# A DeltaNet and SwiGLU kernel: compact state, quadrant products on it, a third K buffer and another order of the output products

## The chip, the cores and the metric

The kernel runs on one core of a Trainium2 chip. The metric is the device time of one execution in microseconds (us). Times come from unprofiled runs; beside them stands one execution that the hardware profiler recorded.

The engines are named as the profile names them: PE is TensorE (matrix products), PEld its weight loads, DVE is VectorE, ACT is ScalarE, POOL is GpSimd, SP is SyncE, which here issues nearly all DMA transfers. L728 means line 728 of the kernel.

## The reference

The first half is a DeltaNet layer: for each of 4 x 8 heads a 48 x 48 state runs through 768 time steps. The second half is a SwiGLU network on the 3072 resulting tokens.

```python
k_n = k / (np.linalg.norm(k, axis=-1, keepdims=True) + 1e-06)
for t in range(S):                      # S = 768, D = 48, B = 4, H = 8
    y[:, :, t] = einsum('bhd,bhde->bhe', q[:, :, t], state)
    v_old = einsum('bhde,bhd->bhe', state, k_n[:, :, t])
    state = state + bt * einsum('bhd,bhe->bhde', k_n[:, :, t], v[:, :, t] - v_old)
...
x = attn_out.transpose(0, 2, 1, 3).reshape(B * S, H * D)     # 3072 x 384
xn = x / np.sqrt(np.mean(x * x, axis=-1, keepdims=True) + 1e-06) * rms_g
g = xn @ w_gate                          # 384 x 1536
out = (g * sigmoid(g) * (xn @ w_val)) @ w_out               # 1536 x 384
```

## The kernel before

The sequence is cut into 12 chunks of 64 steps. Within a chunk the recurrence is solved in closed form: the keys are normalised and transposed, their mutual products K K form a triangular matrix, its inverse (scaled by beta) is the matrix M, and then

- R = V - K S, where S is the state at the chunk's start (`ks`, L728, and the two subtractions L736),
- U = M R (`mr`, L761; copied to `u_` by L812 on ScalarE and L814 on VectorE),
- Y = Q S + P U, where P is the masked product Q K (`qs`, L774, and `pu`, L791, in the same PSUM banks),
- S = S + K U (`ku`, L895, and the four additions L904; chunk 0 copies with L906).

Y then gets its root mean square: squares with a running sum on ScalarE (L835), the power on GpSimd (L843 to L845), scaling on ScalarE into `yn` (L850), transposes on TensorE (L860) and the multiplication by `rms_g` on VectorE into `xf` (L863). For the products of the SwiGLU, seven sums of parts of `xf` are made (L881). A corner of `yn`, called `zz`, also serves in the making of M: the product L668 is copied there and read by L690.

All 32 heads are worked on at once. Two heads with even and odd index sit above each other in 64 partitions each; the buffers `kt` and `qt` (transposed K and Q) hold such pairs, and index d in the code is the upper or lower head of a pair. The state `sbd` is block-diagonal: for each pair a 128 x 96 block with the two 48-wide states on its diagonal and zeros off it, so that one product with 128 rows serves both heads. A product with 64 columns and 128 rows (128*64 in the profile) takes half of TensorE's array; one with 64 rows and 64 columns (64*64) takes a quadrant of it. Each fp32 product is two instructions in the profile.

The SwiGLU of chunks 0 and 1 is done plainly (`ffn_plain`, L922 and L940) while the weights are still being converted from 64-bit to 32-bit words on VectorE and ScalarE (L327 to L368, L348). From chunk 2 on a scheme with fewer products is used: `ffn` makes 15 products per half (L1033), collected in `tmp` (L1043 on VectorE, L1045 on ScalarE), with the silu on ScalarE (L1049) and the product into `hf` on VectorE (L1050). `down` then makes seven products (L1089) instead of eight from sums of `hf` and of the output weights: `sums` (L1082) makes s1 (in the tile `xp1`) and s2 (in `tmp`), rewrites a(1,0) in `hf`, and later rewrites s1; products are read by copies `snap` (L1094) and additions `add` (L1098), and stored. x, y and z_ are the three PSUM banks of these products.

The order of the instructions on every engine is fixed when the kernel is built. Each operation is handed to a planner (`P.add`) with an engine, an estimated duration, a priority and the buffers it reads and writes; the planner plays the whole program through once, always taking the operation that can start first and, among those, the one with the lowest priority value, and deals out the eight PSUM banks on the way (`Group`). Priorities are due times from `due(c, lead)`, a chunk's SwiGLU being due at 160 + PERIOD x (c - 2). On the chip nothing is reordered: an instruction that waits holds up everything behind it on its engine. DMA transfers are issued from SP's queue, in that order too.

In the steady part the attention of one chunk is woven into the SwiGLU products of an earlier one.

Of the kernel before, what the change touches and what calls it, by code (L numbers as in the profile page):

```python
# [129 lines left out]
def kernel(  # L130
# [55 lines left out]
    NK, NKQ = 2, 2  # L186
# [25 lines left out]
    sbd = sbt("sbd", [128, 16, 2, D])  # L212
# [35 lines left out]
    PERIOD = 52.5  # L248
# [6 lines left out]
    def setup():  # L255
        for t, key, pr in ((k2[0], ("k2p", 0), 0), (k2[1], ("k2p", 1), 1), (q2, "q2p", 1)):
            P.add("DVE", V(128), lambda t=t: nc.vector.memset(t[:, :, D:DP], 0.0), pr, w=[key])
# [21 lines left out]
        for keys, t in (  # L279
            ([("m1bd", g, bb) for g in range(2) for bb in range(2)], m1bd),  # L280
            ([("x2bd", y_) for y_ in range(4)], x2bd),
            ([("sbd", d, g) for d in range(2) for g in range(2)], sbd),
        ):
            n = 1
            for e in t.shape[1:]:
                n *= e
            P.add("POOL", 0.05 + 0.0009 * n, lambda t=t: nc.gpsimd.memset(t, 0.0), 1, w=keys)
# [140 lines left out]
    def kkeys_(c):  # L428
        return [("k2", c % NK, 0), ("k2", c % NK, 1)]
# [277 lines left out]
    def recur(c):  # L707
# [6 lines left out]
        sk = [("sbd", d, g) for d in range(2) for g in range(2)]  # L714
# [3 lines left out]
        rk = [("r", p) for p in range(2)]  # L718
        if c:
            psk = [Group(), Group()]  # L720

            def ks():
                for p in range(2):
                    for j in range(2):
                        for g in range(2):
                            for bb in range(2):
                                u = 4 * bb + 2 * p + j
                                nc.tensor.matmul(  # L728
                                    psk[p].t[64 * bb : 64 * bb + 64, 0:DM].rearrange("t (j d g e) -> t j g d e", j=2, d=2, g=2)[:, j, g],
                                    kt[ikq][:, u, 64 * g : 64 * g + 64],  # L730
                                    sbd[:, 2 * u + g],
                                )

            P.add("PE", 1.5, ks, pr, r=ktk + sk, w=psk + rk, ps=psk)
            for p in range(2):
                P.add("DVE", V(384), lambda p=p: nc.vector.tensor_tensor(  # L736
                    out=r_[:, 8 * p : 8 * p + 8], in0=vt[:, 8 * p : 8 * p + 8],
                    in1=psk[p].t[:, 0:DM].rearrange("s (h e) -> s h e", e=D), op=ALU.subtract,
                ), pr, r=vk + [psk[p]], w=[("r", p)], last=psk[p])
# [11 lines left out]
        def groups(d, h):  # L751
            return [d[i, h[0]] for i in range(2)]
# [14 lines left out]
        def qs():  # L767
            for p in range(2):
                for j in range(2):
                    for g in range(2):  # L770
                        for bb in range(2):
                            u = 4 * bb + 2 * p + j
                            n = 192 * p + 96 * j
                            nc.tensor.matmul(  # L774
                                psy[g, p].t[64 * bb : 64 * bb + 64, n : n + 96],
                                qt[:, u, 64 * g : 64 * g + 64],
                                sbd[:, 2 * u + g].rearrange("p d e -> p (d e)"),
                                start=(p == 0 and j == 0),
                                stop=False,
                                skip_group_check=True,  # L780
                            )

        def pu(h):
            for p in h:
                for y_ in range(4):
                    for g in range(2):
                        for bb in range(2):
# [7 lines left out]
                                start=(c == 0 and p == h[0] and y_ == 0),  # L795
# [19 lines left out]
        if c == 1:  # L815
            gy = groups(psy, (0, 1))
            P.add("PE", 1.5, qs, pr, r=qk + sk, w=gy, ps=gy)
        for h in halves:
            gy = groups(psy, h)

            def yy(h=h):
                if c > 1:
                    qs()
                pu(h)

            P.add("PE", 0.6 * len(h) + (1.4 if c > 1 else 0.0), yy, py, r=qk + sk + ptk + uk(h), w=gy, ps=gy)
# [3 lines left out]
        for h in halves:  # L830
            gy = groups(psy, h)

            for g in range(2):
                for p in h:
                    P.add("ACT", A(192) + 0.2, lambda p=p, g=g: nc.scalar.activation(  # L835
                        out=yn[:, p, 192 * g : 192 * g + 192], in_=psy[g, p].t[:, 192 * p : 192 * p + 192], func=ACTF.Square,
                        scale=1.0 / math.sqrt(DM), accum_out=ms[i2][:, p, g : g + 1],
                    ), py, r=[psy[g, p]], w=[("yn", p), ("ms", i2, p)], last=psy[g, p])
            cols = slice(h[0], h[-1] + 1)

            def root(cols=cols):
                m = ms[i2][:, cols, 0]
                nc.gpsimd.tensor_tensor(out=m, in0=m, in1=ms[i2][:, cols, 1], op=ALU.add)  # L843
                nc.gpsimd.tensor_scalar_add(m, m, 1e-6)
                nc.gpsimd.tensor_tensor(out=rs[i2][:, cols], in0=m, in1=mhalf[:, cols], op=ALU.pow)  # L845

            P.add("POOL", 1.1, root, py, r=["half"], w=[(k_, i2, p) for p in h for k_ in ("ms", "rs")])
            for g in range(2):
                for p in h:
                    P.add("ACT", A(192), lambda p=p, g=g: nc.scalar.activation(  # L850
                        out=yn[:, p].rearrange("s (y g e) -> s y g e", g=2, e=D)[:, :, g],
                        in_=psy[g, p].t[:, 192 * p : 192 * p + 192].rearrange("s (y e) -> s y e", e=D),
                        func=ACTF.Copy, scale=rs[i2][:, p : p + 1],
                    ), py, r=[psy[g, p], ("rs", i2, p)], w=[("yn", p)], last=psy[g, p])
# [29 lines left out]
        if c < NCH - 1:  # L884
# [12 lines left out]
            P.add("PE", 1.2, ku, py + 2, r=kkeys_(c) + [("k2p", c % NK)] + uk((0, 1)), w=pss + sk, ps=pss)  # L897
            for g in range(2):
                for d in range(2):
                    s = slice(64 * d, 64 * d + 64)  # L900
                    dst = sbd[s, g:16:2, d]
                    src = lambda s=s, g=g: pss[g].t[s, 0:DM].rearrange("s (u e) -> s u e", e=D)
                    if c:
                        P.add("DVE", V(384), lambda dst=dst, f=src: nc.vector.tensor_tensor(out=dst, in0=dst, in1=f(), op=ALU.add), py + 2, r=[pss[g]], w=[("sbd", d, g)], last=pss[g])  # L904
                    else:
                        P.add("DVE", V(384), lambda dst=dst, f=src: nc.vector.tensor_copy(out=dst, in_=f()), py + 3, r=[pss[g], ("xp", 0), ("xp", 1)], w=[("sbd", d, g)], last=pss[g])  # L906
# [164 lines left out]
    def down(c, start):  # L1071
# [42 lines left out]
        product(y, s1, s1k, wsum[:, 0], True, 4)  # L1114
        snap(p5, y, ["p5"])
        sums(a(1, 0), a(0, 0), a(1, 0), ALU.subtract, ak(0, 0), ak(1, 0), 0, 6)
        product(x, s2, s2k, wsum[:, 1], False, 6)
        snap(u2, x, [("tmp", 0)])
        sums(s1, a(0, 1), s2, ALU.subtract, ak(0, 1) + s2k, s1k, 0, 6)
        product(y, s1, s1k, b(1, 1), False, 8)  # L1120
        add(0, 1, u2, y, [("tmp", 0)])
        store(0)
        product(x, a(1, 0), ak(1, 0), b(0, 1), False, 10)
        add(1, 1, p5, x, [("tmp", 2), "p5"])
# [88 lines left out]
```

## Time and profile before

| | us |
|---|---|
| median of 3 runs | 755.35 (754.93 to 755.64) |
| the profiled execution's own time | 754.56 |
| its span, first to last instruction | 752.8 |
| PE busy in the span | 728.9 |
| DVE busy | 588.6 |
| ACT busy | 293.6 |
| POOL busy | 194.0 |
| mean granted TensorE clock | 0.995 of full speed |

Busy times are sums of one engine's instructions. Products on TensorE are pipelined, and the ends of their records overlap with the next start, so the distance from one start to the next says what a batch of products takes. In lists of waits the first name is who waited, the name behind the arrow is who ended the wait, followed by us in total, the number of times and the longest.

### The profile page before, as it was taken

The page shows a single profiled execution, that of the slowest core. Times are in us where ns is not written, and L with a number is a line of the kernel's source. Part 1 is how long each engine was busy: PE and PEld are TensorE (multiplying, and loading weights), DVE is VectorE, ACT ScalarE, POOL GpSimd, SP SyncE. Part 2 cuts the span into 40 slices and gives each one's busy share as a digit, 9 for nine tenths or more (in the row PEclk, how much of TensorE's full clock was granted, in tenths as well). Part 3 has the DMA queues.
Part 4 walks back from the last instruction along what each step waited for, and adds up shares of the span by engine and source line. Part 5 has one row for each costly group of instructions (what it writes and reads, how often), then busy time and mean ns, then how long its engine had stood idle before and what let it go on. Part 6 is the DMA issues. An engine that isn't in the chain of part 4 may idle for free.

```text
span 752.8 us, 22292 instructions
## 1 busy us (share of the span) xinstructions
PE 728.9 (97%) x9538; PEld 670.5 (89%) x9538; DVE 588.6 (78%) x1145; ACT 293.6 (39%) x718; POOL 194.0 (26%) x197
## 2 busy tenths in 40 slices
PE   9999995999999999999999999999999999999996
PEld 8887774877789999999999999999999999999996
DVE  4999999996955975995986896986885986975463
ACT  3425444123334425425425435335345345244231
POOL 5102205143233131331431431332233233100000
PEclk9999998999999999999999999999999999999999
DMA  7848477032344033224224224233233232030000
GB/s 171 213 73 238 126 179 201 1 55 60 64 77 102 1 63 73 45 46 90 44 43 94 44 46 91 44 61 75 52 66 63 54 68 58 13 61 2 22 1 22
DMA packets 206995, 54.60 MB, mean 73 GB/s; under 512 B 199216, under 2 KB 202288, under 8 KB 206896
## 3 DMA queue, kind: packets, MB, share of 16 engines
q1 hardware_dynamic: 201552, 52.19, 32.8%
q10 hardware_dynamic: 5344, 0.98, 0.8%
q8 instruction: 75, 1.23, 0.7%
q14 instruction: 24, 0.20, 0.1%
HBM read 40.83 MB, written 12.32 MB: 71 GB/s over the span
## 4 chain that ended last, share of the span: by engine, by line
PE 79%; DVE 18%; issue 2%; POOL 1%; ACT 0%; DVEq 0%; POOLq 0%
PE bank L1033 35%; PE bank L1089 12%; PE bank L940 7%; PE bank L1179 5%; PE bank L922 3%; DVE acc L593 3%; PE bank L420 2%; DVE acc L587 2%; PE bank L728 2%; PE bank L397 2%; PE bank L774 2%; DVE xp L1082 2%; DVE tmp L1043 2%; PE bank L761 2%; PE bank L690 1%
## 5 line engine op out<-in xcount | busy, mean ns | idle before, releaser
L1033 PE MATMUL bank<-xf,w_in 128*128 128x128 f32 x1440 | 187.1, 278 | 0.4 <-issue 0.4
L1033 PEld LDWEIGHTS bank<-xf,w_in 128*128 128x128 f32 x1440 | 172.1, 192 | 5.1 <-issue 2.0
L1043 DVE TENSOR_TENSOR tmp<-tmp,bank 128x512 f32<-128x512 f32 x180 | 121.8, 685 | 68.9 <-PE bank L1033 51.9
L1033 PE MATMUL bank<-xf,more 128*128 128x128 f32 x960 | 122.9, 276 | 0.3 <-DVE tmp L1043 0.3
L1033 PEld LDWEIGHTS bank<-xf,more 128*128 128x128 f32 x960 | 115.2, 192 | 1.3 <-DVE tmp L1043 0.5
L1045 ACT COPY tmp<-bank 128x512 f32<-128x512 f32 x120 | 70.2, 586 | 108.9 <-PE bank L1033 107.8
L593 DVE TENSOR_REDUCE acc<-acc 128x30 f32<-128x90 f32 (+4 forms) x180 | 85.0, 472 | 6.2
L1049 ACT ACTIVATE tmp<-tmp 128x256 f32<-128x256 f32 x120 | 50.2, 418 | 89.5 <-DVE tmp L1043 89.4
L1050 DVE TENSOR_TENSOR hf<-tmp 128x256 f32<-128x256 f32 x120 | 62.3, 527 | 28.2 <-ACT tmp L1049 27.1
L440 POOL TENSOR_TENSOR knrm<-ksum,half 128x16 f32<-128x16 f32 x12 | 35.3, 2943 | 144.2 <-DVE ksum L439 144.1
L587 DVE TENSOR_TENSOR acc<-acc,at 128x60 f32<-128x60 f32 (+4 forms) x180 | 63.6, 353 | 7.7 <-POOL at L570 4.4
L1089 PE MATMUL bank<-wo_sb,hf 128*128 128x192 f32 x360 | 64.2, 328 | 2.1 <-DVE hf L1050 2.1
L540 POOL TENSOR_TENSOR at<-at,beta_b 128x1024 f32<-128x1024 f32 x10 | 23.6, 2362 | 160.3 <-DMA at<-dkk 160.3
L1089 PEld LDWEIGHTS bank<-wo_sb,hf 128*128 128x128 f32 x360 | 58.3, 190 | 2.9 <-DVE hf L1050 2.5
L1179 PE MATMUL bank<-ident 128*128 128x128 f32 x314 | 40.5, 290 | 1.4 <-POOL ident masks.py:199 1.4
L940 PE MATMUL bank<-xp,w_in 128*128 128x256 f32 x144 | 34.9, 396 | 6.7 <-DVE xp L863 6.7
L1179 PEld LDWEIGHTS bank<-ident 128*128 128x128 f32 x314 | 38.8, 205 | 2.0 <-POOL ident masks.py:199 1.4
L940 PEld LDWEIGHTS bank<-xp,w_in 128*128 128x128 f32 x144 | 28.4, 200 | 12.5 <-DVE xp L863 7.0
L464 POOL TENSOR_TENSOR pt<-pt,mask_p 128x512 f32<-128x512 f32 x20 | 28.0, 1419 | 41.0 <-ACT pt L463 41.0
L922 PE MATMUL bank<-wo_sb,hf 128*128 128x384 f32 x96 | 35.2, 495 | 0.0
L940 PE MATMUL bank<-xf,w_in 128*128 128x256 f32 x144 | 33.8, 382 | 0.0
L940 PEld LDWEIGHTS bank<-xf,w_in 128*128 128x128 f32 x144 | 27.0, 190 | 5.8 <-issue 0.2
(165 smaller groups left out, 1121.1 us busy)
## 6 DMA issues: line engine op xcount, KB each, us to landing
at<-dkk SPq DMA_DIRECT2D x23, 256.0 KB, 3.9
more<-in_moe_w_gate_dram SPq DMA_DIRECT2D x6, 768.0 KB, 5.5
q<-in_q_dram SPq DMA_DIRECT2D x24, 192.0 KB, 4.2
more<-in_moe_w_val_dram SPq DMA_DIRECT2D x6, 768.0 KB, 4.9
vt<-in_v_dram SPq DMA_DIRECT2D x24, 192.0 KB, 3.7
more<-in_moe_w_out_dram SPq DMA_DIRECT2D x6, 768.0 KB, 6.6
out_dram<-tmp SPq DMA_DIRECT2D x48, 96.0 KB, 2.2
k<-in_k_dram SPq DMA_DIRECT2D x23, 192.0 KB, 4.0
```

The costliest lines, as they stand in the source:

```text
L440: P.add("POOL", 2.95, lambda: nc.gpsimd.tensor_tensor(out=knrm[i2], in0=ksum[i2], in1=half, op=ALU.pow), pn, r=[("ksum", i2), "half"], w=[ ...
L587: nc.vector.tensor_tensor(out=acc[:, 1:3, 0:n, j + 2 : W].rearrange("p a i t -> p i a t"), in0=acc[:, old, 0:n, j : j + 2, None].to_broadc ...
L593: nc.vector.tensor_reduce(out=acc[:, new, 0:n, j + 2 : W], in_=acc[:, lo : lo + 3, 0:n, j + 2 : W].rearrange("p a i t -> p i t a"), axis=A ...
L922: nc.tensor.matmul(po[p].t[:, 0:DM], hf[:, spot(f), 128 * p : 128 * p + 128], wo_sb[:, spot(f)], start=(f == f0), stop=(f == f1 - 1), skip ...
L940: nc.tensor.matmul(ps.t[:, TOK * side : TOK * side + TOK], w_in[:, side, h_, 3 * t + i_, n : n + 128], x_[:, 2 * t : 2 * t + 2].rearrange( ...
L1033: nc.tensor.matmul(g.t[:, 128 * z : 128 * z + 128], fac[:, side, 128 * f : 128 * f + 128], xf[:, xs], start=(begin and z == 0), stop=False ...
L1043: P.add("DVE", V(512), lambda t=t, g=g: nc.vector.tensor_tensor(out=t, in0=t, in1=g.t, op=ALU.add), -1, r=[g], w=[tk], last=g)
L1045: P.add("ACT", A(512), lambda t=t, g=g: nc.scalar.copy(t, g.t), -1, r=[g], w=[tk], last=g)
L1049: P.add("ACT", A(256), lambda t=t: nc.scalar.activation(out=t[:, 0:256], in_=t[:, 0:256], func=ACTF.Silu), -1, w=[tk])
L1050: P.add("DVE", V(256), lambda t=t, f0=f0, p=p: nc.vector.tensor_tensor(out=hf[:, spot(f0) : spot(f0) + 2, 128 * p : 128 * p + 128], in0=t[ ...
L1089: nc.tensor.matmul(g.t[:, 0:192], a_[:, f], b_[:, f], start=(begin and f == 0), stop=(f == 5), skip_group_check=True)
L1179: nc.tensor.matmul(warm[:, 0:128], ident, ident)
```

## The change

- The state is kept in `state`, 128 x 16 x 48, without the zeros: the upper head of a pair in partitions 0 to 63, the lower in 64 to 127. K U is added to it by two operations on 128 partitions instead of four on 64.
- K S and Q S are one function, `on_state`: for each pair and head a product of 64 rows and 64 columns on 48 elements, going round the four quadrants; the results of the upper and lower heads lie in two PSUM banks, and `by_d` picks the matching columns.
- Q S is its own operation with its own two banks. ScalarE copies it into `yn`, and the result of P U is added there by VectorE. From chunk 1 on the squares read `yn`, two of 384 elements instead of four of 192, the scaling is two operations within `yn`, and GpSimd adds no partial sums.
- K has three buffers instead of two.
- PERIOD goes from 52.5 to 50.5.
- In `down` the seven products and their sums come in another order.

```diff
-    NK, NKQ = 2, 2
+    NK, NKQ = 3, 2
-    sbd = sbt("sbd", [128, 16, 2, D])
+    state = sbt("state", [128, 16, D])
-    PERIOD = 52.5
+    PERIOD = 50.5
...
-            psk = [Group(), Group()]
-            def ks():
-                ...
-                nc.tensor.matmul(
-                    psk[p].t[64 * bb : 64 * bb + 64, 0:DM].rearrange(...)[:, j, g],
-                    kt[ikq][:, u, 64 * g : 64 * g + 64],
-                    sbd[:, 2 * u + g],
-                )
-            P.add("PE", 1.5, ks, pr, r=ktk + sk, w=psk + rk, ps=psk)
+            psk, psq = [Group(), Group()], [Group(), Group()]
+            def on_state(t, ps):
+                for x_ in range(4):
+                    for g in range(2):
+                        for d in range(2):
+                            for bb in range(2):
+                                rows, u, n = slice(64 * d, 64 * d + 64), 4 * bb + x_, 96 * x_ + 48 * g
+                                nc.tensor.matmul(
+                                    ps[d].t[64 * bb : 64 * bb + 64, n : n + 48],
+                                    t[rows, u, 64 * g : 64 * g + 64],
+                                    state[rows, 2 * u + g],
+                                )
+            P.add("PE", 1.1, lambda: on_state(kt[ikq], psk), pr, r=ktk + sk, w=psk + rk, ps=psk)
...
+            P.add("PE", 1.1, lambda: on_state(qt, psq), pr, r=qk + sk, w=psq, ps=psq)
+            for d in range(2):
+                P.add("ACT", A(384), lambda d=d: nc.scalar.copy(
+                    by_d(yn.rearrange("s p n -> s (p n)"), d), psq[d].t[:, 0:DM].rearrange("s (x n) -> s x n", x=4)
+                ), py, r=[psq[d]], w=[("yn", p) for p in range(2)], last=psq[d])
...
-        def qs():
-            ...
-            def yy(h=h):
-                if c > 1:
-                    qs()
-                pu(h)
-            P.add("PE", 0.6 * len(h) + (1.4 if c > 1 else 0.0), yy, py, r=qk + sk + ptk + uk(h), w=gy, ps=gy)
+            P.add("PE", 0.6 * len(h), lambda h=h: pu(h), py, r=ptk + uk(h), w=gy, ps=gy)
...
+                for g in range(2):
+                    P.add("DVE", V(384), lambda g=g: nc.vector.tensor_tensor(
+                        out=yn...[:, :, g], in0=yn...[:, :, g],
+                        in1=gy[g].t[:, 0:DM].rearrange("s (y e) -> s y e", e=D), op=ALU.add,
+                    ), py, r=[gy[g]], w=[("yn", p) for p in range(2)])
+                for p in range(2):
+                    P.add("ACT", A(384) + 0.2, lambda p=p, gy=gy: nc.scalar.activation(
+                        out=gy[p].t[:, 0:DM], in_=yn[:, p], func=ACTF.Square, scale=1.0 / math.sqrt(DM), accum_out=ms[i2][:, p, 0:1],
+                    ), py, r=[("yn", p)], w=[gy[p], ("ms", i2, p)], last=gy[p])
...
+                for p in range(2):
+                    P.add("ACT", A(384), lambda p=p: nc.scalar.mul(yn[:, p], yn[:, p], rs[i2][:, p : p + 1]), py, ...)
...
-                for d in range(2):
-                    s = slice(64 * d, 64 * d + 64)
-                    dst = sbd[s, g:16:2, d]
+                dst = state[:, g:16:2]
...
         product(z_, a(0, 1), ak(0, 1), b(1, 0), True, 2)
         add(0, 0, p1, z_, [("tmp", 0)])
-        product(y, s1, s1k, wsum[:, 0], True, 4)
+        product(x, s2, s2k, wsum[:, 1], False, 4)
+        snap(u2, x, [("tmp", 0)])
+        product(y, s1, s1k, wsum[:, 0], True, 6)
         snap(p5, y, ["p5"])
         sums(a(1, 0), a(0, 0), a(1, 0), ALU.subtract, ak(0, 0), ak(1, 0), 0, 6)
-        product(x, s2, s2k, wsum[:, 1], False, 6)
-        snap(u2, x, [("tmp", 0)])
         sums(s1, a(0, 1), s2, ALU.subtract, ak(0, 1) + s2k, s1k, 0, 6)
-        product(y, s1, s1k, b(1, 1), False, 8)
+        product(x, a(1, 0), ak(1, 0), b(0, 1), False, 8)
+        add(1, 1, p5, x, [("tmp", 2), "p5"])
+        product(y, s1, s1k, b(1, 1), False, 10)
         add(0, 1, u2, y, [("tmp", 0)])
         store(0)
-        product(x, a(1, 0), ak(1, 0), b(0, 1), False, 10)
-        add(1, 1, p5, x, [("tmp", 2), "p5"])
         product(x, a(1, 1), ak(1, 1), wsum[:, 2], False, 12)
```

In the profile of the old kernel the seven products of one `down` appear by their tiles: `wo_sb,hf` (a(0,0), then a(0,1)), `wsum,xp` (s1), `wsum,tmp` (s2), `wo_sb,xp` (the rewritten s1), `wo_sb,hf` (a(1,0)) and `wsum,hf` (a(1,1)).

In the changed kernel as built, the planner puts Q S right behind K S in most chunks, and K S of a chunk in chunks 3, 5 and 8 to 11 soon behind K U of the chunk before: K U, the products Q K, one to three batches of the SwiGLU, K S, Q S. In the kernel before some ten batches lie between the two.

## The prediction

> **What bounds the kernel now.** I read the page first: busy shares, then the chain that ended last.
>
> ```profile
> PE 728.9 (97%) x9538; PEld 670.5 (89%) x9538; DVE 588.6 (78%) x1145; ACT 293.6 (39%) x718; POOL 194.0 (26%) x197
> ...
> PE 79%; DVE 18%; issue 2%; POOL 1%; ACT 0%; DVEq 0%; POOLq 0%
> ```
>
> TensorE is busy almost all the time and carries the chain; VectorE carries 18% of it. The windows by stage say where each of them does so (columns: length, then busy time of PE, PEld, DVE, ACT, POOL):
>
> ```profile
> 83.80:129.83 46.03, 37.31 (x584) 29.03 (x582) 44.60 (x69) 21.84 (x49) 14.61 (x11) 0.97 0.65 162
> 129.83:216.70 86.87, 86.87 (x780) 68.43 (x781) 74.62 (x146) 20.48 (x54) 28.24 (x27) 0.98 0.24 45
> ...
> 502.70:557.77 55.07, 54.21 (x781) 52.31 (x782) 44.70 (x90) 23.50 (x59) 17.10 (x18) 1.00 0.32 61
> ```
>
> Up to 129.83 us VectorE is full (44.60 of 46.03) and TensorE has holes. From there on TensorE is full, and a steady period of one chunk is 55.07 us long with 54.21 of TensorE work. The waits of TensorE from 129.8 us on are short enough to list:
>
> ```profile
> PE bank L940 <- DVE xp L863: 6.7, 1, 6.7
> PE bank L1089 <- DVE xp L1082: 5.0, 6, 0.9
> PE bank L1089 <- DVE hf L1050: 2.1, 2, 1.1
> PE bank L1089 <- DVE tmp L1098: 0.4, 1, 0.4
> ```
>
> The first is the end of the startup (TensorE restarts at 129.83 when chunk 1's x is there); the second is six waits, one per chunk, for the third `sums` of `down`. So after 129.83 a microsecond taken from TensorE's list, or from these waits, comes off the end, unless a new wait takes it back. The price of a batch is read from starts in TensorE's timeline, not from busy times, which overlap:
>
> ```profile
> 502.63 1.54 PE L728 MATMUL bank<-sbd,kt 128*64 128x96 f32 x32
> 504.10 1.16 PE L1033 MATMUL bank<-xf,w_in 128*128 128x128 f32 x8
> ...
> 521.83 1.15 PE L761 MATMUL bank<-r,mt 64*64 64x48 f32 x64
> 522.91 1.16 PE L1033 MATMUL bank<-xf,w_in 128*128 128x128 f32 x8
> ...
> 524.89 1.54 PE L774 MATMUL bank<-sbd,qt 128*64 128x96 f32 x32
> 526.36 1.15 PE L791 MATMUL bank<-u,pt 64*64 64x48 f32 x64
> 527.33 1.11 PE L895 MATMUL bank<-u,k 64*64 64x48 f32 x64
> 528.37 1.09 PE L397 MATMUL bank<-ident,q 128*128 128x128 f32 x8
> ...
> 540.97 2.19 PE L1089 MATMUL bank<-wo_sb,xp 128*128 128x192 f32 x12 [0.86 <-DVE xp L1082]
> ```
>
> K S (L728) and Q S (L774) take 1.47 us each from start to next start; 64 instructions of 64x48 in quadrants take 1.08 (L761, after full-array products), 0.97 (L791) and 1.04 (L895).
>
> **Quadrant products.** Each of K S and Q S becomes 64 instructions of 64x48, the very form and quadrant order of L791. K S, behind full-array products, is priced like L761: 1.08. Q S follows K S as built, so like L791 and L895: 1.0. P U loses its neighbour and becomes the first quadrant batch: 0.97 to 1.08, a loss of 0.11. After the restart there are ten K S (chunks 2 to 11): 10 x 0.39 = 3.9. Nine Q S: 9 x 0.47 = 4.2. P U: 10 x 0.11 = 1.1 back. The tenth Q S, of chunk 2, no longer waits for P U of its own chunk; as built it stands ahead of chunk 1's transposes (L860), in the 6.7 us hole, and its whole 1.47 leaves the full stretch. Sum: 3.9 + 4.2 - 1.1 + 1.47 = 8.5. Bounds: all new batches at 1.09 (L420, 64 instructions) gives 7.7; all at 0.97 and no loss on P U gives 11.0. I take 8.5, as L761, L791 and L895 are the same shape.
>
> A rule speaks against this part. The Trainium skill, TensorEngine Tiling (Array Packing), section Instruction Overhead, says that a matmul has about 60 cycles of overhead, so that a short free dimension costs as much as 60, and not to take the tiling factor from a dimension that is already small. By it twice the instructions at 48 would cost 64 x 60 against 32 x 96, 1.25 times as much: an estimate of 1.84 us a batch instead of 1.47, and 7 us lost over the nineteen batches. The rows of L791 and L895 have the very shape, and go by 1.0, so the sum stays with the rows.
>
> **Order of the output products.** Before, the product on the rewritten s1 (`wo_sb,xp`) stands 1.95 us after the last reader of s1 (`wsum,xp`), and VectorE needs the 0.94 us rewrite behind queued work: 0.86 of wait. As built, `wo_sb,hf` on a(1,0) now lies between, with `wsum,tmp` ahead of `wsum,xp`. VectorE's queue between (two L863 at 0.55, some L881 at 0.43, one step of the inverse at 1.0, the rewrite 0.94) ends about 0.8 us before its reader. So the 5.0 goes, and so does the 0.4 at the very end (L1098 read the bank that the last product writes; another product lies between now). The price is that `wsum,tmp` is due one product earlier and needs s2; its last third, the only part that waits for the last tiles, starts 1.3 us into the product, and I cost that at nothing (0 to 4 us over all chunks). One of the two L1050 waits (1.0, first SwiGLU chunk) goes too, since another product, a weight product and the transposes lie between now. Sum: 6.4, bounds 3 to 6.5.
>
> **Compact state.** Two state additions on 128 partitions replace four on 64 (L904, 0.55 each: it is elements per partition that count), and two additions of Q S to P U (about 0.55, like L736) come. VectorE per chunk: -1.1 + 1.1 = 0. ScalarE gets two copies of 384 (0.48, L812), two squares and two scalings of 384 instead of four each of 192 (0.33 + 0.21 and 0.43): about +0.5 us, and it is busy 23.5 of 55.07. GpSimd loses one 0.28 addition. The chain from P U to the transposes of y grows by the two additions: additions 1.2, squares 1.4, GpSimd 1.0, scalings 1.0, with hand-overs some 5.5 us, and as built 7 to 8 us of TensorE work lie over it. Setup swaps a GpSimd memset for a small VectorE one, under the K load: 0, at most 0.2 if uncovered. In the full VectorE stretch before 129.83, chunk 0's four copies become two, chunk 1's four additions two, and two come: -1.1. But GpSimd's mask products and its scaling of `at` run there and stretch two-input VectorE work:
>
> ```profile
> 122.74 2.98 DVE L333 SCALAR_TENSOR_TENSOR wo_sb<-more,wo_sb 128x768 uint32<-128x768 uint32 x1
> 125.76 1.97 DVE L338 TENSOR_SCALAR more<-wo_sb 128x768 uint32<-128x768 uint32 x1
> ```
>
> (0.96 and 0.56 elsewhere). As built the masks come ahead of `at`, so up to 2 us more of the conversions fall under GpSimd. I take -0.5 for the restart, bounds -1.5 to +2.
>
> **Third K buffer.** It moves two DMA issues on SP's queue and the norms earlier, past no new issue of another kind. TensorE waits for no K in the list above: 0. The new PERIOD only shifts due times; what it does is in the built order.
>
> **New waits.** As built, three places are short. In chunk 5's `down`, the product on a(0,1) comes 2.0 us after its last SwiGLU product, and addition 0.69, silu 0.42, product 0.42, with one more L1043 and two steps of the inverse queued ahead, need 3.1: +1.1 (0 to 2). Chunk 6's transposes stand only 3.9 us ahead of its SwiGLU, and VectorE needs two L863, seven L881 (2.5 together), a step of the inverse and an L1098: +1.9 (0 to 2.5). Chunk 11's stand one product (1.95) ahead, with 3.6 of VectorE work: +1.5 (0.5 to 2). And in six chunks (3, 5, 8 to 11) K S now follows K U after 2 to 4 us of other products, while the state additions queue behind the additions of y and the norm's sum (L437, 0.95): I find 0.2 us of slack, cost +0.1 each, 0.6 in all (0 to 6). Sum +5.1.
>
> **Sum.** -8.5 - 6.4 - 0.5 + 5.1 = -10.3. The profiled execution took 754.56 (span 752.8, 1.8 around it), so 744.3 there; the runs' median is 755.35, 0.8 above it, and 745.0 is my number.
>
> **Rivals.** (a) The new waits don't come, because VectorE has room where I queued it: -8.5 - 6.4 - 0.5 = -15.4, 740. For it: VectorE is idle 10 us a period; against: 12.1 of 13 us busy just behind K U in the steady period. (b) The reorder is given back: waits for s2, hf and xf grow to twice my sum and the order gains half: -8.5 - 3.2 - 0.5 + 10.2 = -2, 753. For it: every one of TensorE's late waits already names VectorE. (c) Slower: K S waits for the state. In those six chunks the additions of the state stand behind work that itself waits for P U, the norm's sum and GpSimd-stretched hf products (0.42 rising to 1.56 at the worst). It decides when VectorE comes to the y additions more than 2 us later than P U's end: each chunk then loses 1.8 us or more, 6 x 1.8 = 11, and the gain is gone; at 2.5 us each, 15, with (b)'s half gain of the order and the other new waits (4.5), it ends 7 above the median, near 762. Against: the queue ahead of them is some 3.2 us and starts 2.9 us before P U ends. (d) Nothing changes on TensorE, quadrants being limited per instruction at L728's 46 ns: L791 at 15 ns excludes this.
>
> **Chances.** My sum 0.54, (a) 0.18, (b) 0.19, (c) 0.08, (d) 0.01. The measurement tells 0.2% (1.5 us) from no change. Faster: all of my sum and (a), and most of (b): 0.87; same 0.05; slower 0.08. The range goes from just under (a), 739.0, to inside (b), 751.5; the unknown bounds (7.7 to 11.0, 0.5 to 10 of waits) fit into it.
>
> **What would show it.** Right: L728 and L774 as 64 instructions with starts 1.0 to 1.1 apart, a steady period near 53.4 us, no wait for the third `sums` in the new order, waits of 1 to 2 us for hf in chunk 5 and for xf ahead of chunk 6's and 11's SwiGLU, the restart at 128 to 131. Wrong: K S waiting for the state in each of the six chunks, batches at 1.4 or more, or a restart past 132.

## The result and the profile after

The changed kernel takes 758.2 us (median of 20 runs, 754.6 to 761.1) against 754.8 for the kernel before (20 runs, 753.4 to 756.8): ratio 1.0046, 95% interval 1.0032 to 1.0060. A second series (experiment e12) gives 1.0049 (1.0028 to 1.0070). It is slower by 0.5%, where 745 was forecast. Two executions that took far longer than the rest, one of e16 (1883 us) and one of e17 (1456 us), are in no ratio.

The page of the first profiled execution (754.73 us, span 753.0), the same two lines as of before:

```profile
PE 720.5 (96%) x10212; PEld 661.8 (88%) x10212; DVE 593.9 (79%) x1146; ACT 297.0 (39%) x674; POOL 189.8 (25%) x185
...
PE 68%; DVE 25%; issue 4%; POOL 2%; ACT 1%; DVEq 0%; POOLq 0%
```

TensorE's busy time is 8.4 us less. But its share of the chain fell from 79% to 68%, and VectorE (18% to 25%) and "issue" (2% to 4%) took it over. Two steady periods, in the windows by stage, hold less work in about the same time:

```profile
494.88:549.84 54.96, 53.32 (x844) 51.68 (x843) 44.97 (x91) 24.11 (x55) 16.41 (x16) 1.00 0.32 62
549.84:605.42 55.58, 53.58 (x843) 51.45 (x843) 45.55 (x90) 23.98 (x55) 16.43 (x16) 1.00 0.25 47
```

53.4 was forecast for the period, 55.07 was the old one. Line numbers of the changed kernel differ from the old ones: L728 is now both K S and Q S, L770 is M R, L784 P U, L896 K U, L419 Q K, L939 `ffn_plain`, L1032 `ffn`, L1088 `down`; on VectorE L903 adds to the state, L1042 to `tmp`, L1049 makes `hf`, L1081 are the `sums`. The next view is the string of quadrant batches in TensorE's timeline of the first profile:

```profile
530.18 1.15 PE L784 MATMUL bank<-u,pt 64*64 64x48 f32 x64
531.15 1.11 PE L896 MATMUL bank<-u,k 64*64 64x48 f32 x64
532.08 1.11 PE L419 MATMUL bank<-qt,kt 64*64 64x64 f32 x58
534.39 0.34 PE L419 MATMUL bank<-qt,kt 64*64 64x64 f32 x6 [1.20 <-issue]
...
535.75 1.15 PE L728 MATMUL bank<-state,kt 64*64 64x48 f32 x64
536.72 0.98 PE L728 MATMUL bank<-state,qt 64*64 64x48 f32 x50
538.13 0.44 PE L728 MATMUL bank<-state,qt 64*64 64x48 f32 x14 [0.43 <-issue]
```

K S starts 0.97 before Q S, less than the 1.08 that was forecast. Q S, at the end of the string, takes 1.78 to the next start (538.50), more than the old 1.47. Twice TensorE stops in the middle of a batch, and the profile shows nothing that it waits for ("issue").

That first profile is one of the fastest runs. The second (e12, span 757.8) is nearer the median, and its waits of TensorE from the restart on are:

```profile
PE bank L939 <- DVE xp L864: 4.3, 1, 4.3
PE bank L1088 <- DVE xp L1081: 3.3, 4, 1.4
PE bank L419 <- issue: 3.1, 3, 1.3
PE bank L1088 <- DVE hf L1049: 2.9, 3, 1.3
PE bank L1032 <- DVE tmp L1042: 2.4, 2, 1.2
PE bank L728 <- issue: 2.0, 4, 1.0
PE bank L728 <- DVE state L903: 1.7, 2, 1.2
PE bank L784 <- DVE u L807: 1.4, 1, 1.4
```

From these lists and the windows, in us (waits below 0.15 are in no list):

| | before | after, first profile | after, second |
|---|---|---|---|
| restart at | 129.83 | 126.23 | 130.16 |
| restart to end | 623.0 | 626.8 | 627.6 |
| TensorE busy in it | 610.1 | 604.1 | 602.3 |
| "issue" waits in it | 0.4 | 5.2 | 5.1 |
| waits for the third sums | 5.0 | 1.9 | 3.3 |
| all other listed waits | 3.2 | 10.8 | 12.1 |

By the second profile: 7.8 less work, 4.7 more "issue", 1.7 less for the third sums, 8.9 more of other waits: +4.1 of the 4.6 that the stretch grew. Busy time also grows where the granted clock is at half, which it is for 4.0 us of the stretch before, 6.8 of it in the first profile and 3.4 in the second. Taking off half of these, an estimate, leaves 7.4 and 7.5 less work in the two.

### The profile page after: what moved, and what is told of

Its sections match the earlier page's. It is cut to its first block, busy times and chain, and to the rows that moved or that the text cites. A ratio compares the mean times of both kernels' runs of the same rounds, so it can differ in the third digit from the quotient of the medians.

```text
span 753.0 us, 23603 instructions
## 1 busy us (share of the span) xinstructions
PE 720.5 (96%) x10212; PEld 661.8 (88%) x10212; DVE 593.9 (79%) x1146; ACT 297.0 (39%) x674; POOL 189.8 (25%) x185
## 4 chain that ended last, share of the span: by engine, by line
PE 68%; DVE 25%; issue 4%; POOL 2%; ACT 1%; DVEq 0%; POOLq 0%
PE bank L1032 33%; PE bank L1088 14%; DVE acc L592 4%; DVE acc L586 3%; PE bank L939 3%; DVE hf L1049 3%; PE bank L1178 2%; PE bank L419 2%; DVE tmp L1042 2%; PE bank L396 2%; PE bank L921 2%; PE bank L728 2%; PE bank L689 1%; PE bank L770 1%; DVE w_in L332 1%
## 5 line engine op out<-in xcount | busy, mean ns | idle before, releaser
L1042 DVE TENSOR_TENSOR tmp<-tmp,bank 128x512 f32<-128x512 f32 x180 | 122.4, 685 | 80.9 <-PE bank L1032 66.8
L1032 PE MATMUL bank<-xf,w_in 128*128 128x128 f32 x1440 | 182.1, 277 | 0.4 <-ACT tmp L1044 0.4
L1032 PEld LDWEIGHTS bank<-xf,w_in 128*128 128x128 f32 x1440 | 170.0, 192 | 4.3 <-issue 1.4
L1032 PE MATMUL bank<-xf,more 128*128 128x128 f32 x960 | 125.4, 277 | 2.4 <-DVE tmp L1042 2.4
L1032 PEld LDWEIGHTS bank<-xf,more 128*128 128x128 f32 x960 | 115.6, 192 | 4.3 <-DVE tmp L1042 2.8
L1049 DVE TENSOR_TENSOR hf<-tmp 128x256 f32<-128x256 f32 x120 | 70.6, 591 | 19.5 <-ACT tmp L1048 18.2
L1088 PE MATMUL bank<-wo_sb,hf 128*128 128x192 f32 x360 | 66.0, 334 | 3.7 <-DVE hf L1049 3.3
L586 DVE TENSOR_TENSOR acc<-acc,at 128x60 f32<-128x60 f32 (+4 forms) x180 | 66.4, 369 | 3.4
L1088 PEld LDWEIGHTS bank<-wo_sb,hf 128*128 128x128 f32 x360 | 59.9, 194 | 5.0 <-DVE hf L1049 4.0
L1178 PE MATMUL bank<-ident 128*128 128x128 f32 x284 | 37.2, 291 | 1.4 <-POOL ident masks.py:199 1.4
L1178 PEld LDWEIGHTS bank<-ident 128*128 128x128 f32 x284 | 35.5, 205 | 2.5 <-POOL ident masks.py:199 1.4
L939 PE MATMUL bank<-xp,w_in 128*128 128x256 f32 x144 | 34.6, 395 | 3.1 <-DVE xp L864 3.1
L939 PEld LDWEIGHTS bank<-xp,w_in 128*128 128x128 f32 x144 | 28.3, 198 | 9.0 <-DVE xp L864 3.3
L613 POOL COPY acc<-acc 128x128 f32<-128x128 f32 x40 | 16.4, 448 | 72.3 <-DVE acc L592 72.3
L939 PE MATMUL bank<-xf,w_in 128*128 128x256 f32 x144 | 34.2, 383 | 0.0
L1093 ACT COPY tmp<-bank 128x192 f32<-128x192 f32 x30 | 9.4, 318 | 57.9 <-PE bank L1088 50.6
```

The lines of the kernel that those rows point to most:

```text
L586: nc.vector.tensor_tensor(out=acc[:, 1:3, 0:n, j + 2 : W].rearrange("p a i t -> p i a t"), in0=acc[:, old, 0:n, j : j + 2, None].to_broadc ...
L939: nc.tensor.matmul(ps.t[:, TOK * side : TOK * side + TOK], w_in[:, side, h_, 3 * t + i_, n : n + 128], x_[:, 2 * t : 2 * t + 2].rearrange( ...
L1032: nc.tensor.matmul(g.t[:, 128 * z : 128 * z + 128], fac[:, side, 128 * f : 128 * f + 128], xf[:, xs], start=(begin and z == 0), stop=False ...
L1042: P.add("DVE", V(512), lambda t=t, g=g: nc.vector.tensor_tensor(out=t, in0=t, in1=g.t, op=ALU.add), -1, r=[g], w=[tk], last=g)
L1049: P.add("DVE", V(256), lambda t=t, f0=f0, p=p: nc.vector.tensor_tensor(out=hf[:, spot(f0) : spot(f0) + 2, 128 * p : 128 * p + 128], in0=t[ ...
L1088: nc.tensor.matmul(g.t[:, 0:192], a_[:, f], b_[:, f], start=(begin and f == 0), stop=(f == 5), skip_group_check=True)
```

## The experiments

Theories, by the names used in the expectations: T1, strings of quadrant batches outrun the supply of instructions. T2, VectorE comes late for what the new order and the new additions ask of it. T3, the shorter PERIOD spoils the planner's order. T5, waits halve TensorE's granted clock for a while. Where the planner's costs or rules are touched, the whole built order moves.

**One part alone, or one part undone (e1 to e4).**

e1 is the kernel before with only the `down` hunk of the change.

> The kernel before with the new order of the seven output products and nothing else (block-diagonal state, two K buffers, PERIOD 52.5 stay). Theory T1, instruction supply: what ate the gain is strings of quadrant batches (P U, K U, Q K, K S, Q S) that outrun the instructions; this kernel keeps the 32 wide products for K S and Q S, so it should bring my full term for the order: the 5.0 us of waits for the third sums and 0.4 at the end go, no more 'issue' waits than before's 1.8 us in all, and the median falls by 4 to 6.5 us against the kernel before (ratio 0.991 to 0.995). Theory T2, VectorE comes late: the new order asks for s2, hf and the last output sum earlier, and the waits for them grow by what the old one lost: ratio 0.998 to 1.004, with 4 us or more of waits for hf, s2 and the adds in the list.

Measured 759.4, ratio 1.0045 (1.0027 to 1.0064): the order alone makes it slower. Its profile, TensorE and then VectorE in one steady `down`:

```profile
594.54 2.11 PE L1089 MATMUL bank<-wsum,xp 128*128 128x192 f32 x12
596.49 2.11 PE L1089 MATMUL bank<-wo_sb,hf 128*128 128x192 f32 x12
599.08 2.19 PE L1089 MATMUL bank<-wo_sb,xp 128*128 128x192 f32 x12 [0.48 <-DVE xp L1082]
```

```profile
596.72 1.01 DVE L863 TENSOR_TENSOR xf<-bank,g_sb 128x384 f32<-128x384 f32 x2
...
597.98 0.95 DVE L1082 TENSOR_TENSOR xp<-hf,tmp 128x768 f32<-128x768 f32 x1
```

The rewrite of s1 may start when `wsum,xp` has read it, about 596.6, and its reader is due at 598.4. The rewrite ends at 598.93, 0.5 too late. One product lies between the two, as in the kernel before, with `wsum,tmp` there (`wsum,xp` at 536.04, `wsum,tmp` at 537.99, reader at 540.97). The reader moved back by one product and so did the last read. These waits total 4.2 instead of 5.0, and those for the additions L1098 and for L1043 grew from 0.7 to 2.3.

e2 is the changed kernel with the old product order and:

```diff
-    NK, NKQ = 3, 2
+    NK, NKQ = 2, 2
-    PERIOD = 50.5
+    PERIOD = 52.5
```

> The changed kernel with the old order of products, two K buffers and PERIOD 52.5, so the compact state with quadrant K S and Q S alone. In the built order only a few chunks have five quadrant batches in a row (K S stands 5 or more SwiGLU products behind K U in all but the last chunk). T1: the quadrant price is right (K S and Q S 1.0 to 1.1 instead of 1.47) and little is lost to supply: 'issue' waits below 4 us after 126 us of the span, the five waits for the third sums (about 5 us) still there; ratio 0.986 to 0.993 (8.5 for the quadrants, 3 from the earlier restart, less 1 to 2). T2 (the additions of Q S and the state load VectorE at the wrong places): waits for state, xf and hf grow by 6 us or more here too; ratio 0.996 to 1.004.

Measured 766.0, ratio 1.0144 (1.0118 to 1.0169), worse than either theory said. In its built order the products of `down` wait for the additions that read their bank:

```profile
PE bank L1088 <- DVE tmp L1097: 9.3, 7, 2.6
```

and the restart comes at 134.67, after waits of 1.35 for the state, 2.8 for yn and 6.2 for chunk 1's x, with the clock at half from 123.1 to 140.2. The work itself is 7.0 shorter after the restart (603.1 against 610.1).

e3 undoes only the product order, e4 only PERIOD (52.5).

> The changed kernel with the old order of the seven products; state, third K buffer and PERIOD 50.5 as changed. The five quadrant batches stand in a row in chunks 8 and 11 only; Q S still follows K S at once. T1: the waits for the third sums come back (+5 us), and some 2 to 3 us of 'issue' waits go: ratio to the kernel before 1.005 to 1.010. T2, the new order is what makes VectorE late: the waits for hf, state and the sums go with it, ratio 0.990 to 0.998.

> The changed kernel with PERIOD 52.5 as before; all else as changed. Theory T3, the shorter period makes the planner push attention ahead, into the shadow of the SwiGLU of the chunk before, and this makes K S wait for the state and the strings: at 52.5 the ratio to the kernel before falls under 0.997, with state waits under 1 us. T1 and T2: the built order has as many strings (K S two products or less behind Q K in chunks 3, 5, 7, 9 and 11), so the time stays within 2 us of the changed kernel's, ratio 1.002 to 1.007.

Measured 765.1, ratio 1.0124 (1.0106 to 1.0142), and 766.6, ratio 1.0142 (1.0122 to 1.0162). Neither lies in a range that T1 or T2 gave. T3 has the wrong sign: with the other parts in place, the new order and PERIOD 50.5 are worth some 6.9 and 8.4 us by the medians. In e3 the waits for hf are 8.0 in all, in e4 the "issue" waits 7.9 after the restart (13.4 in the whole span). So in these orders no part is good or bad by itself; each built order has its own set of waits.

**Instruction supply (e8, e6, e9).**

e8 appends products to the kernel before:

```diff
+        for w_, n in ((48, 1024), (96, 512)):
+            for i in range(n):
+                d, bb, x_ = i % 2, i // 2 % 2, i // 4 % 4
+                nc.tensor.matmul(banks[6 + d][64*bb : 64*bb+64, 96*x_ : 96*x_+w_], kt[0][64*d : 64*d+64, 4*bb + x_, 0:64], ...)
```

> The kernel before with products appended after its last one, on operands that lie ready, results used by nobody: 1024 quadrant products of 64x48, then 512 of 64x96. T1: the first 100 to 200 of the short ones go at 15 ns each, then instruction supply sets in at about 27 ns (256 instructions, 128 products, per 16 KB fetch of 3.4 to 4.1 us), so the 1024 take 26 to 30 us with 'issue' waits; the 512 wide ones go at about 31 ns, 16 us, without such waits. Rival (no supply limit): 15 ns throughout, 15.5 to 17 us for the 1024 and as much for the 512.

e8 was run once. The expectation counted products where the profile has two records for each; its prices are those of a record. Measured:

```profile
747.68 3.59 PE L1186 MATMUL bank<-r,kt 64*64 64x48 f32 x230
752.25 2.08 PE L1186 MATMUL bank<-r,kt 64*64 64x48 f32 x128 [0.97 <-issue]
...
810.53 2.87 PE L1186 MATMUL bank<-r,kt 64*64 64x96 f32 x128 [0.60 <-issue]
```

230 records go at 15.6 ns, then 128 at a time, a new lot every 3.47 to 4.02 us: 27 to 31 ns a record. 128 records with their weight loads are 256 instructions, one 16 KB packet of the instruction queue, and in the trace each hole ends some 1.2 to 1.5 us after such a packet lands. T1's mechanism holds, and the wide products, against the expectation, are held back too (22.4 ns each when they run, but 3.47 to 3.75 us per lot). Five batches in a row are 320 records.

e6, same order, K S and Q S in half as many records:

```diff
-                    for g in range(2):
...
-                                nc.tensor.matmul(ps[d].t[..., n : n + 48], t[rows, u, 64 * g : 64 * g + 64], state[rows, 2 * u + g])
+                            nc.tensor.matmul(ps[d].t[..., 96 * x_ : 96 * x_ + 96], t[rows, u, 0:64], state[rows, 2 * u : 2 * u + 2])
```

> The changed kernel, same order on every engine, but K S and Q S go as 32 quadrant products on 96 elements instead of 64 on 48: half the instructions for the same streamed columns (the odd heads take their neighbour's keys, so this leaves part of the computation out). T1: the strings are five batches long as before but hold 256 fewer instructions of 1280 in fifths, so 'issue' waits after the restart fall from 6.8 to 3.5 us or less, starts of K S and Q S stay about 1.0 apart, and the median falls by 2.5 to 5 us, to 753 to 756. Rival: the 'issue' waits are semaphores or banks that the profile does not show; they stay at 5 to 8 us, and the median within 1.5 us of 758.

Measured 752.6, ratio 0.9967 (0.9949 to 0.9984):

```profile
535.02 0.89 PE L727 MATMUL bank<-state,kt 64*64 64x96 f32 x32
535.73 0.84 PE L727 MATMUL bank<-state,qt 64*64 64x96 f32 x32
536.50 1.09 PE L396 MATMUL bank<-ident,q 128*128 128x128 f32 x8
```

This proves less than was meant: a batch of 32 wide records takes 0.71 to 0.83 from start to start, not 1.0, so some 5 of the 5.6 us are plain work. The holes in K S and Q S (3.5 in the first profile) are gone; those in Q K, ahead of them in the string, are not. The "issue" sum after the restart is 4.9, and not the 3.5 or less that T1 said.

e9 teaches the planner the supply:

```diff
+                    if e == "PE" and s > 130.0:
+                        s = max(s, t_tok + (need(op) - tok) / 33.0)    # need: 64 for a quadrant batch
```

> The changed kernel with one rule more in the planner, and nothing else: a batch of 64 quadrant instructions may start only when a store of 105 instructions, refilled at 33 per us, holds 64 (as measured in the string experiment: 128 per 3.6 us). From chunk 2 on the built order then has P U, K U, one to three products of the SwiGLU or the output, Q K, another one or two, K S, Q S. T1: 'issue' waits after the restart fall from 5.2 us to 1.5 or less, and the median falls by 3 to 5 us, to 753 to 755.5. Rival (the holes only cover other waits): the 'issue' waits go, but waits for state, hf or xp grow by as much, median 757 or more.

Measured 764.4, ratio 1.0128 (1.0109 to 1.0146). The strings are broken and the "issue" waits after the restart fall from 5.2 to 1.5, as T1 said. The rival has the time: waits that the changed kernel does not have come in (lines stand 7 lower here: L1095 is a product of `down`, L871 the multiplication into xf, L868 the transposes of y),

```profile
PE bank L1095 <- DVE xf L871: 4.9, 3, 2.6
...
PE bank L868 <- ACT yn L862: 1.5, 1, 1.5
```

and behind two of them (1.95 and 2.57 us) the clock halves.

**VectorE relieved (e5, e7, e13, e14; e15 to e17).** The first four cut the seven sums of xf to 4 columns from chunk 3 on, in the changed kernel, in e1, in e9 and in the kernel before:

```diff
-                    out=dst, in0=a, in1=b_, op=op
+                    out=dst[..., 0:w_], in0=a[..., 0:w_], in1=b_[..., 0:w_], op=op     # w_ = 4
```

> The changed kernel, every instruction in the same order on every engine, but the seven sums of parts of xf (L881, 2.5 us of VectorE per chunk) run on 4 of 128 columns from chunk 3 on, so about 1.8 us less of VectorE per chunk just where its queue is full; this leaves part of the computation out. T2 (VectorE comes late): the waits for hf, xp, tmp and state after the restart, 14.6 us in the changed kernel's profile (5.0 + 3.3 + 3.3 + 2.5 and 0.5 for u; 3.1 of them the restart itself), fall to 6 us or less, and the median falls by 4 to 8 us to 750 to 754. T1 (instruction supply): the 'issue' waits of 6.8 us stay within 1.5 us of that, and the median falls by less than 3 us.

> The kernel before with the new order of products alone (759.4 us), same order of instructions, with the sums L881 cut to 4 columns from chunk 3 on (part of the computation left out). T2: the new order gains nothing because VectorE is full in the stretch of the output products and the rewrite of s1 comes as late as the order asks for it; with 1.8 us a chunk less there, the waits for the third sums fall from 4.2 (plus 1.3 for L1098 and 1.0 for L1043) to under 1.5 in all and the median to 750 to 754. T1 and T5 (the clock): the waits hardly fall, 757 or more.

> The kernel of the supply experiment (planner with the store of instructions) with the sums L881 cut to 4 columns as in the light experiment (part of the computation left out): both sinks relieved. If each sink only hands its time to the other: 'issue' waits 1.5 us or less after the restart, waits for VectorE 10 us or less (15.4 in the changed kernel, about 20 in the supply experiment), median 748 to 753, 5 us or more under the changed kernel's 758. Rival (neither is what holds the kernel; the loss is in chains of latency through PSUM banks, ScalarE and VectorE, whatever the queue's length): VectorE waits 13 us or more, median 755 or more.

> The kernel before with the sums L881 cut to 4 columns from chunk 3 on (part of the computation left out). With the same cut the new order of products took 752.6 us. If the order is worth its 5 us where VectorE has room, this kernel keeps its waits for the third sums and stays at 755 to 758. If VectorE's queue was the cause of those waits, they go here too (5.0 to under 1.5 us), the median is 749 to 752.5, and the order is worth nothing or less in either case.

Measured 756.9, 752.6, 761.0 and 752.9 us; ratios 1.0014 (0.9996 to 1.0031), 0.9959 (0.9947 to 0.9972), 1.0075 (1.0049 to 1.0101) and 0.9960 (0.9944 to 0.9975). The relief was put in the wrong place. In e14 the reader of the third sums still waits 4.7 in all, since only one of the seven sums stands ahead of the rewrite in VectorE's queue. What two of the four do show: with this relief the order of products alone is worth nothing (e7's 752.6 against e14's 752.9).

The last three cut the steps of the inverse, which do stand ahead of it, in the changed kernel, in the kernel before and in e9's:

```diff
-            def step(j=j, n=n, m=m):
+            def step(j=j, n=1 if c >= 3 else n, m=m):
```

> The changed kernel, same order of instructions, with the steps of the inverse from chunk 3 on cut to one row block instead of up to 15 (part of the computation left out), some 6 us less of VectorE per chunk. If VectorE's lateness eats the gain: its waits after the restart fall from 15.4 to 7 us or less, the 'issue' waits stay near 5, and the median falls by 5 to 9 us to 749 to 753. Rival (chains of latency): waits for VectorE stay at 11 or more, median 755 or more.

> The kernel before with the same cut of the inverse (part of the computation left out). Its waits for the third sums (5.0) stand behind these steps and go, to 1 us or less; median 749 to 752. With e15 this gives the worth of the whole change where VectorE has room: the shorter work of TensorE (8) less instruction supply (4.7) says that e15 is 1 to 4 us faster than this; if e15 is no faster, the change is worth nothing even then.

> The kernel of the supply experiment with the same cut of the inverse (part of the computation left out): strings broken up and VectorE relieved. If these two are all that eats the gain: 'issue' 1.5 us or less, VectorE waits 8 or less after the restart, median 744 to 749, 3 us or more under e15. Rival: the order that the planner makes here is what costs (its waits of 2 to 2.6 us for xf ahead of the product on s1, which ScalarE's scaling of yn makes late): 753 or more.

Measured 750.3 (ratio 0.9941, 0.9922 to 0.9959), 748.2 (0.9905, 0.9886 to 0.9924) and 748.3 (0.9911, 0.9895 to 0.9927). The changed kernel's list after the restart in e15, then that of e16:

```profile
PE bank L1088 <- DVE hf L1049: 2.8, 4, 1.1
PE bank L419 <- issue: 2.8, 3, 1.1
PE bank L728 <- issue: 2.3, 4, 0.7
PE bank L728 <- DVE state L903: 2.0, 2, 1.2
```

```profile
PE bank L1089 <- DVE hf L1050: 1.9, 2, 1.1
PE bank L1089 <- DVE xp L1082: 0.7, 1, 0.7
```

The third sums are gone from e15's list and nearly from e16's: VectorE's queue made those waits. The lighter queue took 7.8 us off the changed kernel (758.0 to 750.3), but 6.8 off the kernel before as well, so the change stays 2 us behind. What is left in e15 is above all instruction supply (5.1) and two waits as long as in the second profile: hf, through ScalarE's silu (2.8 against 2.9), and the state behind K U (2.0 against 1.7). e17 takes the supply out too (0.9), and is 2.0 us faster than e15: breaking up the strings pays where VectorE has room. But it is no faster than e16. TensorE's busy time after the restart is 9.3 less there than in e16 (600.6 against 609.9), and waits other than for supply are 10.2 against 3.0, with these at the head of e17's list:

```profile
PE bank L1095 <- DVE hf L1056: 3.7, 4, 1.3
PE bank L791 <- DVE u L814: 1.9, 2, 1.2
PE bank L1095 <- DVE xf L871: 1.6, 2, 0.8
PE bank L868 <- ACT yn L862: 1.4, 1, 1.4
PE bank L1095 <- DVE state L910: 1.3, 3, 0.6
```

So with both relieved, waits along chains through VectorE and ScalarE still take the gain.

**The clock (e10, e11, e12).** In the first profile of the changed kernel the granted clock is at half from 365.36 to 368.77, right after a wait of 1.48 for hf; the product behind it took 3.90 instead of 2.1. e10 and e11 put useless products into waits of the changed kernel (at the restart, and in chunks 4 and 11 ahead of the product on a(0,1)) and of the kernel before (at the restart):

```diff
+                    for z in range(8 if c == 1 and f == 0 and side == 0 else 0):      # e11: 22
+                        nc.tensor.matmul(ps.t[:, 128 * (z % 4) : 128 * (z % 4) + 128], ident, ident)
```

> The changed kernel, same order, with useless products of 128x128 on the identity put into three waits: 8 before chunk 1's first product at the restart (3.1 us of wait), 5 before the product on a(0,1) of chunk 4 (1.5 us of wait), 4 before that of chunk 11 (1.1). Theory T5: a wait of 1.5 to 3 us halves the granted clock for 3.4 us or a multiple, 1.7 us of loss each; with the waits filled the profile shows no half clock at chunk 4 and at most 3.4 us of it around the restart, the mean clock of the runs rises from 0.992 to 0.995 or more, and the median falls by 1.5 to 4 us. Rival (the clock falls for another reason): mean clock unchanged within 0.001, median the same or up to 1 us more for the products that come too late.

> The kernel before with 22 useless products of 128x128 (about 4.9 us) in its wait of 6.7 us ahead of chunk 1's first product. T5: the half clock from 127.0 to 133.8 us of the span goes, of which 4.0 us lie behind the restart, so the median falls by 1.5 to 2.2 us (ratio 0.997 to 0.998), the mean clock rises by 0.004. Rival: the products delay the restart or the clock falls all the same: ratio 0.999 to 1.003.

> The changed kernel as it is, for a second profile and the spread of its runs on this chip: ratio to the kernel before 1.003 to 1.007 as before. T1 and T5 say that its runs differ among themselves by the number of windows of half clock, each 1.7 us and 0.0023 of mean clock, and by the length of the hole in the string of chunk 1 (1.6 us in the first profile, 3.2 to 3.9 in three variants that hold the same string): runs of clock 0.995 and more at 754 to 757, of 0.991 and less at 758 to 761.

e10: 760.4, ratio 1.0078 (1.0065 to 1.0091), clock 0.991 to 0.995: missed, and 2.3 us slower than e12, the changed kernel in the same series. There was no half clock at chunk 4, but e12 had none there either without any filling; the clock fell at 118.1 instead, within the hole of 4.3 us in chunk 1's string, and once more at 165.9. e11: 753.2, ratio 0.9986 (0.9974 to 0.9998), clock 0.996 to 1.000, no half clock but at the end: a gain of 1.1 us, somewhat less than the 1.5 to 2.2 expected, and the only version here, with the whole computation, below the kernel before. e12: clock alone does not sort the changed kernel's runs (at 0.995 they lie from 755.9 to 759.5), while in e1 it does: 756.5 to 756.6 at 0.995, 759.4 to 761.0 at 0.991 to 0.993. The other part of the spread is in e12's own timeline of chunk 1:

```profile
120.22 0.78 PE L896 MATMUL bank<-u,k 64*64 64x48 f32 x20 [3.40 <-issue]
...
130.16 5.19 PE L939 MATMUL bank<-xp,w_in 128*128 128x256 f32 x15 [4.26 <-DVE xp L864]
```

The packet of instructions that ends this hole landed at 118.8; in the first profile the one with the same place in the queue had landed at 113.7, and the restart came at 126.23. Of the ten other profiles with this string all but e2's have the hole, at 3.2 to 4.3 us.

## Why the prediction was wrong

By the second profile the span grew by 5.0 us where 10.3 less was forecast. Of these 15.3, new waits on other lines have 5.2, instruction supply 4.7, the third sums 3.3, the restart 0.8 and TensorE's work 0.7; 0.6 is in no list.

- **Quadrants: right about the work, with a term left out.** The sum put 8.5 on the stretch after the restart; busy time there fell by 6.0 in the first profile and 7.8 in the second (7.4 and 7.5 with the clock taken off, as above). K S was priced at 1.08 and is 0.97. The 1.0 for Q S holds for a batch whose instructions are there; at the end of the string above Q S costs 1.78, and 2.33 in the second profile. The prediction took its rows from batches that stand two or three together, and asked of its 128 instructions, twice as many as before, only what they do to the array. Their supply was put at nothing without a reason; it is 4.7 us.
- **The rule that was set aside.** The Trainium skill, TensorEngine Tiling (Array Packing), section Instruction Overhead, says that a product with a free dimension of 1 takes as long as one with 60. e8 agrees in kind: a record takes 16.3 ns with 48 elements and 22.4 with 96, so the short one costs 0.73 of the long one and not half. The comparison that mattered, against 46 ns for the old 128-row form, still went as the prediction said.
- **Product order: the step whose mechanism failed.** The -6.4 rested on another product lying between s1's last reader and the reader of its rewrite. But `wsum,tmp`, which lay there before, had moved ahead of `wsum,xp`: one product between them in both orders. VectorE's rewrite was to end 0.8 us ahead of its reader; in e1 it ends 0.5 after the reader is due. Of the 5.0, 3.3 stayed in the second profile (1.9 in the first, 4.2 in e1), and with the order alone the kernel got slower.
- **New waits: less than half of their size, and other places.** 5.1 was forecast, or 3.7 net of the 1.4 that the order was to save outside the third sums; all waits but supply and third sums grew by 8.9, from 3.2 to 12.1. The 1.1 for hf in chunk 5 was 0.2, but chunk 4's, not foreseen, was 1.3 to 1.5; no wait for xf came ahead of chunks 6 and 11, while L1042, `u` and s2 took 4.7 together. K S waited for the state in two chunks, not six: rival (c)'s mechanism, at 1.7 us where it had 11.
- **Restart: -0.5 forecast, -3.6 in a lucky run, +0.3 in a typical one.** As far as these two profiles show, the hole in chunk 1's string (1.64 us in the first, 3.40 in the second) decides whether the additions saved arrive.
- **Rival (b)** was the nearest in kind, the reorder given back, but it allowed the quadrants their full 8.5, with no loss to supply, and so ended at 753.
- **Not settled:** e1's profile is 1.9 us above before's, its median 4.4; the clock covers most of the rest. Why the chain through hf is late in chunks 4 and 11 above all (1.3 and 1.1 in the second profile) was not taken apart, nor why e17's chains are longer than e16's.

## What to carry to other kernels

Where one engine is busy 97% of the time, a per cent taken off its list is only a gain as far as the chains that run beside it have slack: measure the neighbours' slack first, for instance by making VectorE's largest work cheaper and looking which waits go. Before crediting a reorder, count the instructions between the last reader and the next reader in both orders. Count instructions as a resource as well as columns: splitting products into quadrants pays while a batch stands alone, and much less in a long string.

## What the runs showed of the hardware

- In e8 TensorE had a reserve of 230 product records (460 instructions with the weight loads); beyond it 256 instructions came every 3.47 to 4.02 us. In the changed kernel's string above the first hole came after 186 records (64 + 64 + 58). While the weights were loading, packets landed 3.5 to 8.2 us apart (e12, from 110.6 to 128.2). The Trainium skill, Runtime: NRT & Kernel Launch, section Instruction fetch mechanics, states the block of 256 instructions, which fits, and that its cost is mostly hidden, which the strings here contradict with holes of 0.3 to 4.3 us.
- The granted clock fell to half for 3.41 us or a multiple of it (6.83, 10.24 and 17.07 in these profiles; stretches at the very end left aside). A wait of 1.48 us was followed by such a window in one run, and the same place with 1.30 was not in another; filling the wait at the restart of the kernel before (e11) took 6.8 us of half clock away and 1.1 us off the time.
